# Reordering the first token chunk of a fused attention and MLP kernel: a later load of the last w_out quarter, output tiles kept open, AV items in score banks

## Chip, cores, metric

One core of one Trainium2 chip. The metric is device time of one launch, in microseconds (us). Ratios are the mean time of one kernel's fast runs over the mean of the other's fast runs of the same rounds on the same chip, so they are not quite the ratio of the medians quoted. Each has a 95% interval. One run of the kernel before (334.01 us) did not count as fast. "PE" is TensorE's matmul row of the profile, "ACT" ScalarE, "DVE" VectorE, "POOL" GpSimd, "SP" the queue that issues output stores.

## The reference, cut

```python
# q, k, v: (8 batches, 8 heads, 576, 64); s: (8, 8, 576)
scores = q @ k.T / 8 ; bias = -(cumsum(relu(s))_i - cumsum(relu(s))_j) ; causal mask
attn   = softmax(scores + bias) @ v            # per batch and head
x      = attn as (4608 tokens, 512)
h      = x @ w_in                              # 512 x 2048
g      = 0.5 * h * (1 + erf(h / sqrt(2)))
out    = g @ w_out                             # 2048 x 512
```

## The kernel before: the parts that matter

Tokens go through the MLP in nine chunks of 512. Between the output matmuls of chunk c (`l2_item`: 128 matmuls, 4 output tiles of 128 tokens, 16 steps each) the kernel runs the attention of batch c+1 (here "pair" p means heads 2p and 2p+1):

- `tr_items`: PE transposes of q and k, copied out by ScalarE and VectorE;
- `sc_item`: scores, exp on ScalarE (1.02 us each, two per pair), causal masks on VectorE;
- `av_item`: the product with v (numerator `num`) and with the decay weights (denominator `den`), then ln and exp of the denominator on ScalarE and the product into `xT` on VectorE.

The kernel shares the 8 banks of PSUM among three kinds of tile: "sc" (2 tiles of 2 banks, here called score banks), "av" (3 of one), "mlp" (1).

```python
def av_item(b, p, wide=False, rest=True):
    num, den = av_banks(wide)          # wide: both halves of one "sc" tile
    if wide:
        av_mm(b, p, num, MAIN, False)
    av_mm(b, p, den, MAIN, True)
    ln = norm_act(den, CUT, CHUNKS)    # ScalarE: ln, ln, exp
    if not wide:
        av_mm(b, p, num, MAIN, False)
    ...
    norm_dve(b, p, p + 1, num, ln, 0, CUT, CHUNKS)   # VectorE, into xT
...
def l2_item(c, sub, f0=0, f1=FT, av=False, copy=None):
    if f0 == 0:
        tag, bufs = ("av", 3) if av else ("mlp", 1)
        o_of[c, sub] = ps.tile([128, KO * 128], fp32, tag=tag, bufs=bufs, name="o_ps")
    ...                                 # the matmuls of steps f0 to f1
    if f1 < FT:
        return
    o_sb = work.tile([128, KO * 128], fp32, tag="osb", bufs=3, name="o_sb")
    (copy or nc.vector.tensor_copy)(o_sb, o_ps)
    nc.sync.dma_start(out=out[r0 : r0 + 128, :], in_=o_sb)
```

Around chunk 0, GpSimd also re-lays q and k of batch 2. These are four SBUF-to-SBUF copies, called `interleave`; they stand ahead of this stretch in program order and start when the loads are in:

```python
        if c == 0:
            load_v(2)
            interleave(2, "q")         # two GpSimd copies 128 x 1152 bf16
            interleave(2, "k")         # two more
```

Of the kernel before, what the change touches and what calls it, by code (L numbers as in the profile page):

```python
# [19 lines left out]
def kernel(  # L20
# [10 lines left out]
    nc = tc.nc  # L31
# [64 lines left out]
    def early_tile(b, n, p):  # L96
        key = "qk"[p // 2] if b < 2 else n
        if (b, key) not in early:
            early[b, key] = work.tile([128, 2, 2, G * D], bf16, tag=f"raw{key}", bufs=3, name=f"early_{key}")
        return early[b, key], (int(n == "k") if b < 2 else p // 2) * 64  # L100

    def load_early(b, n, p):
        src = q if n == "q" else k
        t, e0 = early_tile(b, n, p)
        nc.gpsimd.dma_start(
            out=t[e0 : e0 + 64].rearrange("g j e f -> g (j e) f"),
            in_=bass.AP(
                tensor=src.tensor,
                offset=src.offset + (b * H + 2 * p) * S * D,
                ap=[[G * D, 64], [S * D, 4], [1, G * D]],  # L110
            ),
        )
# [75 lines left out]
    def write_rows(b, i, eng):  # L188
        rows_of[b, i] = t = dram.tile([2, 2, S, 128], bf16, name=f"rows{b}_{i}")
        eng.dma_start(  # L190
            out=t.rearrange("j a (g r) c -> (a g) j (r c)", r=G),
            in_=qk_of.pop((b, i)).rearrange("p j r e d -> p j (r e d)"),
        )
# [283 lines left out]

    CHUNKS = [(0, 0, 256), (1, 256, CUT)]

    def av_item(b, p, wide=False, rest=True):  # L480
        num, den = av_banks(wide)
        if wide:
            av_mm(b, p, num, MAIN, False)
        av_mm(b, p, den, MAIN, True)
        ln = norm_act(den, CUT, CHUNKS)
        if not wide:
            av_mm(b, p, num, MAIN, False)
        if rest:
            av_rest(b, p)
        norm_dve(b, p, p + 1, num, ln, 0, CUT, CHUNKS)  # L490
# [44 lines left out]
    def l2_item(c, sub, f0=0, f1=FT, av=False, copy=None):  # L535

        gT = gT_of[c]
# [3 lines that stand above are left out]
        o_ps = o_of[c, sub]  # L541
        for ft in range(f0, f1):
            for e in range(2):
                t0 = sub * 128 + e * 64
                nc.tensor.matmul(  # L545
                    o_ps[e * 64 : e * 64 + 64], lhsT=gT[:, ft, t0 : t0 + 64], rhs=w_out_r[:, ft, :],
                    start=(ft == 0), stop=(ft == FT - 1), skip_group_check=True,
# [5 lines that stand above are left out]
        r0 = c * NB + sub * 128  # L553
        nc.sync.dma_start(out=out[r0 : r0 + 128, :], in_=o_sb)
# [56 lines left out]
    nc.gpsimd.tensor_copy(pace, w_in_r[:, 0, 0:1])  # L611
    for n in "qk":
        load_early(1, n, 0)
    for i in range(4):
        load_w(1, i)
    load_v(1)
    for n in "qk":
        load_early(1, n, 2)
    load_qk(2)
    avs = {p: av_banks(p < 2, p == 3) for p in (2, 0, 1, 3)}  # L620
    for p in (2, 0, 1, 3):
# [9 lines left out]
    for c in range(NCH):  # L631
        nb = c + 1
        for k0, k1 in ((0, 2), (2, 3)) if c == 0 else ((0, 3),):
            l1_item(c, 0, k0, k1)
            l1_item(c, 1, k0, k1)
        l1_item(c, 0, KO - 1)
        l1_item(c, 1, KO - 1)
        l1_item(c, 2, av=True)
        if 0 < c and nb < B:
            scale_v(nb, STS, nc.vector)  # L640
            absmax_v(nb)
        if c == 0:
            absmax_v(0)
            scale_v(0, STS[ST - 1 :], nc.vector)
        if c < B:
            for p in range(NP):
                absmax(c, p)
        if 1 < c and nb + 1 < B:
            nc.gpsimd.tensor_copy(pace, qkT[nb % 2][:, 1, NP - 1, 0:1])
            load_v(nb + 1)  # L650
            if nb + 2 < B:
                load_qk(nb + 2)
        for f2 in range(3, FT // 2):
            l1_item(c, f2)
        if c == 0:
            load_v(2)
            interleave(2, "q")
            interleave(2, "k")
            for p in range(NP):
                av_rest(0, p)  # L660
            tr_items(1, 0, (0, 1), wide=True)
            tr_items(1, 1, (0, 1), (nc.scalar.copy, nc.vector.tensor_copy), wide=True)
            exp_set()
            l2_item(c, 0, 0, 4)
            l2_item(c, 1, 0, 4, av=True)
            norm_rest(0)
            l2_item(c, 0, 4, 8)
            sc_item(1, 0)
            l2_item(c, 1, 4, 8, av=True)
            l2_item(c, 0, 8, 12)  # L670
            sc_item(1, 1)
            l2_item(c, 1, 8, 12, av=True)
            l2_item(c, 2, 0, 8, av=True)
            l2_item(c, 0, 12, copy=nc.scalar.copy)
            l2_item(c, 1, 12, av=True)
            scale_pair(1, 0)
            scale_pair(1, 1)
            l2_item(c, 2, 8, av=True, copy=nc.scalar.copy)
            av_item(1, 0, rest=False)
            l2_item(c, 3, 0, 4)  # L680
            tr_items(1, 2, (0, 1), (nc.scalar.copy, nc.vector.tensor_copy), wide=True)
            tr_items(1, 3, (0, 1), (nc.scalar.copy, nc.vector.tensor_copy), wide=True)
            scale_pair(1, 2)
            av_item(1, 1, rest=False)
            scale_pair(1, 3)
            l2_item(c, 3, 4, 8)
            sc_item(1, 2)
            l2_item(c, 3, 8, 12)
            sc_item(1, 3)
            write_rows(2, 0, nc.sync)  # L690
            av_item(1, 2, wide=True, rest=False)
            write_rows(2, 1, nc.sync)
            l2_item(c, 3, 12)
            av_item(1, 3, rest=False)
            for p in (0, 1):
                transpose_rows(2, p)
            gelu_set()
            for p in (2, 3):
                transpose_rows(2, p)
            nc.gpsimd.tensor_copy(pace, qkT[0][:, 1, 3, 0:1])  # L700
            load_qk(3)
            load_v(3)
            absmax_v(1)
        elif nb < B:
            exp_set()
            l2_item(c, 0, 0, 4)
            if c == 1:
                for p in range(NP):
                    av_rest(1, p)
            sc_item(nb, 0)  # L710
            if c == 1:
                norm_rest(1)
            l2_item(c, 0, 4)
            late = c < 3
            for p in range(1, NP):
                if nb + 1 < B and p == 1 and not late:
                    interleave(nb + 1, "q")
                    write_rows(nb + 1, 0, nc.sync)
                if nb + 1 < B and p > 1 and not late:
                    transpose_rows(nb + 1, p - 2)  # L720
                sc_item(nb, p)
                av_item(nb, p - 1)
                if nb + 1 < B and p == NP - 1 and late:
                    interleave(nb + 1, "k")
                    write_rows(nb + 1, 1, nc.sync)
                l2_item(c, p, 0, 12)
                if p == NP - 1:
                    if nb + 1 < B:
                        for pt in range(0 if late else p - 1, NP):
                            transpose_rows(nb + 1, pt)  # L730
                    if c == 1:
                        nc.gpsimd.tensor_copy(pace, qkT[(nb + 1) % 2][:, 1, p, 0:1])
                        load_qk(nb + 2)
                    av_item(nb, p)
                    norm_rest(nb)
                    gelu_set()
                l2_item(c, p, 12)
                if nb == B - 1 and p == 1:
                    cert_decay()
                if nb + 1 < B and p == 2 and late:  # L740
                    interleave(nb + 1, "q")
                    write_rows(nb + 1, 0, nc.sync)
                if nb + 1 < B and p == 1 and not late:
                    interleave(nb + 1, "k")
                    write_rows(nb + 1, 1, nc.sync)
        else:
            if c == B - 1:
                cert_1()
            for sub in range(4):
                if c == NCH - 1 and sub == 2:  # L750
                    break
                l2_item(c, sub, av=sub % 2 == 0)
                if c == B - 1 and sub < 3:
                    (cert_2, cert_3, cert_4)[sub]()
# [174 lines left out]
```

## Time and profile before

| | before |
|---|---|
| median (range), 6 runs | 327.62 us (326.76 to 334.01) |
| span of the profiled run | 324.7 us |
| PE busy | 316.0 us (97%) |
| layer 1 of chunk 0 starts at | 20.31 us |
| layer 1 of chunk 1 starts at | 57.95 us |
| layer 1 of chunk 2 starts at | 92.97 us |

All that the change touches lies between the first and the last of these three starts. I call that distance, 72.66 us here, "the stretch", and use it to compare profiles. From layer 1 of chunk 2 to the start of the last group of matmuls every profile agrees: 220.50 us before, 220.51 after, 220.50 to 220.52 in all the runs below.

### The profile page before, as it was taken

To read this page: it belongs to the slowest core of one execution; us is meant where nothing else is said; L and a number is where in the kernel's file an instruction comes from. 1 tells how busy PE (TensorE), PEld (TensorE's weight loads), DVE (VectorE), ACT (ScalarE), POOL (GpSimd) and SP (SyncE) were. 2 spreads that over 40 slices of the span, in tenths; PEclk is the share of its full clock that TensorE was granted. 3 is DMA by queue.
4 is the path that set the end of the run, shared out by engine and by line. 5 is a ranking of instruction groups with operands and counts; after the bars stand their busy time and mean duration, and the time that the engine had idled before them with its cause. 6 is when DMAs were issued, how large, how long until landed. Compare 5 with 4: busy or idle time off the path is not lost.

```text
span 324.7 us, 8755 instructions
## 1 busy us (share of the span) xinstructions
PE 316.0 (97%) x3755; PEld 183.9 (57%) x3755; DVE 191.1 (59%) x376; ACT 205.0 (63%) x292; POOL 69.8 (21%) x104
## 2 busy tenths in 40 slices
PE   8999998999999999999999999999999999999994
PEld 3666555666655556556655665556555655555554
DVE  6777547995579257936494749655883673150011
ACT  3896749758676857677667767677759676204500
POOL 8745253504300460007105300500000000000000
PEclk9999999999999999999999999999999999999999
DMA  7999999854985799968997996645500110010012
GB/s 113 219 207 209 234 191 266 266 110 51 261 256 112 108 225 253 185 109 250 222 223 145 214 239 141 166 139 177 129 15 34 63 38 2 33 66 34 1 69 71
DMA packets 53837, 47.45 MB, mean 146 GB/s; under 512 B 31328, under 2 KB 43872, under 8 KB 53792
## 3 DMA queue, kind: packets, MB, share of 16 engines
q0 software_dynamic: 15936, 23.07, 39.2%
q1 hardware_dynamic: 37856, 23.75, 27.3%
q8 instruction: 31, 0.51, 0.6%
q14 instruction: 14, 0.11, 0.1%
HBM read 36.85 MB, written 16.52 MB: 164 GB/s over the span
## 4 chain that ended last, share of the span: by engine, by line
PE 81%; DMA 11%; POOL 4%; ACT 2%; issue 1%; DVE 0%; POOLq 0%; DVEq 0%
PE h_ps L523 34%; PE o_ps L545 33%; DMA w_out_r<-in_moe_w_out_dram 5%; PE sc_ps L388 4%; PE avd L426 4%; DMA early_k<-in_k_dram 4%; PE avn L426 3%; DMA w_in_r<-in_moe_w_in_dram 3%; PE lo_ps L769 2%; PE avr L426 1%; POOL raw_v L205 1%; ACT P L404 1%; POOL early_q L117 1%; POOL early_k L117 1%; POOL w_out_r L250 0%
## 5 line engine op out<-in xcount | busy, mean ns | idle before, releaser
L523 PE MATMUL h_ps<-xT,w_in_r 128*64 128x512 bf16 x1152 | 126.2, 379 | 0.1
L545 PE MATMUL o_ps<-w_out_r,gT 128*64 128x512 bf16 x1088 | 125.9, 380 | 0.0
L523 PEld LDWEIGHTS <-w_in_r 128*64 128x64 bf16 x1152 | 68.5, 110 | 55.8 <-issue 0.7
L530 ACT ACTIVATE gT<-h_ps 128x1024 bf16<-128x1024 f32 x54 | 54.3, 1023 | 52.2 <-PE h_ps L523 52.2
L545 PEld LDWEIGHTS <-gT 128*64 128x64 bf16 x1088 | 59.2, 110 | 48.3
L404 ACT ACTIVATE P<-sc_ps 128x1024 bf16<-128x1024 f32 x64 | 62.1, 1021 | 26.2 <-PE sc_ps L388 25.0
L413 DVE TENSOR_TENSOR P<-P,tri_bf 128x512 bf16<-128x512 bf16 x58 | 24.2, 423 | 43.6 <-ACT P L404 43.2
L552 DVE COPY o_sb<-o_ps 128x512 f32<-128x512 f32 x32 | 22.0, 687 | 46.3 <-PE o_ps L545 46.3
L216 DVE TENSOR_REDUCE amx<-qkT 128x2 f32<-128x1152 bf16 x32 | 40.9, 1334 | 0.0
L205 POOL DMA_DIRECT2D raw_v<-in_v_dram x40 | 34.7, 918 | 8.5 <-DMA early_q<-in_q_dram 2.4
L462 DVE SCALAR_TENSOR_TENSOR xT<-avn,ln 128x256 bf16<-128x256 f32 (+3 forms) x66 | 22.4, 386 | 21.3 <-ACT ln L443 15.5
L233 DVE TENSOR_TENSOR vv<-raw_v,wb 128x512 bf16<-128x512 f32 (+3 forms) x44 | 25.2, 630 | 0.0
L223 DVE TENSOR_REDUCE amv<-raw_v 128x1 f32<-128x2048 f32 (+1 forms) x16 | 23.0, 1469 | 2.4 <-DMA raw_v<-in_v_dram 2.4
L443 ACT ACTIVATE ln<-ln 128x512 f32<-128x512 f32 (+1 forms) x40 | 23.5, 587 | 1.3
L533 ACT ACTIVATE gT<-h_ps 128x512 bf16<-128x512 f32 x36 | 19.6, 602 | 6.3 <-PE h_ps L523 6.3
L442 ACT ACTIVATE ln<-avd 128x256 f32<-128x256 f32 x58 | 19.2, 391 | 6.3 <-PE avd L426 6.3
L388 PE MATMUL sc_ps<-qkT 64*128 64x256 bf16 (+2 forms) x320 | 21.1, 250 | 0.7 <-ACT P L404 0.7
L388 PEld LDWEIGHTS <-qkT 64*128 64x128 bf16 x320 | 13.1, 94 | 15.1 <-issue 13.1
L426 PEld LDWEIGHTS <-wb 128*64 128x64 bf16 x384 | 17.1, 110 | 3.9 <-issue 0.3
L426 PEld LDWEIGHTS <-vv 128*64 128x64 bf16 x384 | 17.7, 110 | 1.8 <-issue 1.0
L426 PE MATMUL avd<-P,wb 128*64 128x256 bf16 x232 | 16.5, 263 | 0.0
L426 PE MATMUL avn<-P,vv 128*64 128x256 bf16 x232 | 16.0, 260 | 0.0
(101 smaller groups left out, 164.8 us busy)
## 6 DMA issues: line engine op xcount, KB each, us to landing
out_dram<-o_sb SPq DMA_DIRECT2D x34, 256.0 KB, 3.3
raw_v<-in_v_dram POOLq DMA_DIRECT2D x32, 256.0 KB, 8.6
rows<-qk_bf SPq DMA_DIRECT2D x12, 576.0 KB, 5.9
early_q<-in_q_dram POOLq DMA_DIRECT2D x13, 288.0 KB, 10.3
early_k<-in_k_dram POOLq DMA_DIRECT2D x13, 288.0 KB, 11.7
w_in_r<-in_moe_w_in_dram POOLq DMA_DIRECT2D x4, 512.0 KB, 11.4
w_out_r<-in_moe_w_out_dram POOLq DMA_DIRECT2D x4, 512.0 KB, 15.0
raw_v<-in_v_dram POOLq DMA_DIRECT2D x8, 128.0 KB, 10.2
```

The costliest lines, as they stand in the source:

```text
L205: nc.gpsimd.dma_start(out=t[:n_st, st, :, :], in_=bass.AP(tensor=v.tensor, offset=v.offset + b * H * S * D + st * 128 * D, ap=[[D, n_st], ...
L216: nc.vector.tensor_reduce(amx[:, b * NP + p], qkT[b % 2][:, :, p, :S], axis=AX, op=ALU.max, apply_absolute_value=True)
L223: nc.vector.tensor_reduce(amv[:n_st, b, j : j + 1], t[:n_st, st0:st1].rearrange("p s h d -> p (s h d)"), axis=AX, op=ALU.max, apply_absolu ...
L233: eng.tensor_tensor(vb[:n_st, st0:st1, h0:h1, :], t[:n_st, st0:st1, h0:h1, :], wb[:n_st, st0:st1, b * H + h0 : b * H + h1] .unsqueeze(3).t ...
L388: nc.tensor.matmul(s_ps[:, e, off : off + n], lhsT=qkT[b % 2][e * 64 : e * 64 + 64, 1, p, jt * 128 : jt * 128 + 128], rhs=qkT[b % 2][e * 6 ...
L404: nc.scalar.activation(P[:, :, UO[u] : UO[u] + UW[u]], s_ps[:, :, : UW[u]], func=AF.Exp, scale=scale)
L413: eng.tensor_tensor(d, d, tri_bf.unsqueeze(1).unsqueeze(1).to_broadcast([128, 2, 2, 128]), op=MULT)
L426: nc.tensor.matmul(out[e * 64 : e * 64 + 64, lo : lo + n], lhsT=(wb[:, jt, b * H + h : b * H + h + 1].to_broadcast([128, 64]) if den else ...
L443: nc.scalar.activation(ln[:, :w], ln[:, :w], func=AF.Exp, scale=-1.0)
L523: nc.tensor.matmul(h_of[c, f2][i][e * 64 : e * 64 + 64], lhsT=w_in_r[:, ko, ft * 128 + e * 64 : ft * 128 + e * 64 + 64], rhs=xT[:, ko, c * ...
L530: nc.scalar.activation(gT_of[c][:, f2 * 2 : f2 * 2 + 2, :], hh_of[c, f2], func=AF.Gelu)
L545: nc.tensor.matmul(o_ps[e * 64 : e * 64 + 64], lhsT=gT[:, ft, t0 : t0 + 64], rhs=w_out_r[:, ft, :], start=(ft == 0), stop=(ft == FT - 1), ...
```

## The change

Intent: have v and the last q and k of batch 1 earlier by loading w_out's last quarter behind them. Then use that: run AV of pairs 0 and 1 sooner in score banks, keep all four output tiles of chunk 0 open, and spend their last steps as filler where TensorE waited for ScalarE.

```diff
-    def av_item(b, p, wide=False, rest=True):
+    def av_item(b, p, wide=False, rest=True, den_first=None):
         num, den = av_banks(wide)
-        if wide:
+        den_first = not wide if den_first is None else den_first
+        if not den_first:
             av_mm(b, p, num, MAIN, False)
         av_mm(b, p, den, MAIN, True)
         ln = norm_act(den, CUT, CHUNKS)
-        if not wide:
+        if den_first:
             av_mm(b, p, num, MAIN, False)
@@
-    for i in range(4):
+    for i in range(3):
         load_w(1, i)
     load_v(1)
-    for n in "qk":
-        load_early(1, n, 2)
+    for p in (2, 3):
+        for n in "qk":
+            load_pair(1, n, p)
+    load_w(1, 3)
     load_qk(2)
@@
             l2_item(c, 1, 8, 12, av=True)
-            l2_item(c, 2, 0, 8, av=True)
-            l2_item(c, 0, 12, copy=nc.scalar.copy)
-            l2_item(c, 1, 12, av=True)
+            l2_item(c, 2, 0, 12, av=True)
             scale_pair(1, 0)
             scale_pair(1, 1)
-            l2_item(c, 2, 8, av=True, copy=nc.scalar.copy)
-            av_item(1, 0, rest=False)
-            l2_item(c, 3, 0, 4)
+            av_item(1, 0, wide=True, rest=False, den_first=True)
+            l2_item(c, 3, 0, 4, av=True)
+            av_item(1, 1, wide=True, rest=False, den_first=True)
+            l2_item(c, 3, 4, 8, av=True)
             tr_items(1, 2, ...)              # cut: arguments unchanged
             tr_items(1, 3, ...)
             scale_pair(1, 2)
-            av_item(1, 1, rest=False)
+            l2_item(c, 3, 8, 12, av=True)
+            sc_item(1, 2)
             scale_pair(1, 3)
-            l2_item(c, 3, 4, 8)
-            sc_item(1, 2)
-            l2_item(c, 3, 8, 12)
+            l2_item(c, 0, 12)
+            l2_item(c, 1, 12, av=True)
             sc_item(1, 3)
+            l2_item(c, 2, 12, av=True)
             write_rows(2, 0, nc.sync)
             av_item(1, 2, wide=True, rest=False)
+            l2_item(c, 3, 12, av=True)
             write_rows(2, 1, nc.sync)
-            l2_item(c, 3, 12)
             av_item(1, 3, rest=False)
```

## The prediction

> **What bounds the kernel now.** I read the summary page, then a table of engine busy time by stretch, then the chain of waits, then TensorE's, VectorE's and GpSimd's timelines between 34 and 62 us, then the DMA view in short stretches.
>
> The page and the table by stretch (columns: stretch, its length, then busy us of PE, PEld, DVE, ACT, POOL, granted clock, DMA share, GB/s):
>
> ```profile
> PE 316.0 (97%) x3755; PEld 183.9 (57%) x3755; DVE 191.1 (59%) x376; ACT 205.0 (63%) x292; POOL 69.8 (21%) x104
> ...
> 30.00:40.00 10.00, 9.74 (x188) 6.16 (x186) 6.49 (x8) 7.01 (x10) 3.45 (x5) 1.00 1.23 226
> 40.00:50.00 10.00, 9.94 (x136) 5.49 (x135) 4.59 (x12) 5.41 (x9) 5.14 (x8) 1.00 1.15 200
> 50.00:60.00 10.00, 8.84 (x170) 6.05 (x160) 9.01 (x22) 9.49 (x16) 4.91 (x6) 1.00 0.98 240
> 80.00:90.00 10.00, 10.00 (x134) 6.27 (x132) 5.64 (x16) 6.04 (x10) 4.40 (x6) 1.00 1.10 241
> ```
>
> TensorE is the bound: 8.7 us of the 324.7 us span lack a matmul, and most of these lie before the first matmul (1.2) and after the last (about 4). What the change can reach is the stretch from 34.9 to 58.7 us: the output matmuls of token chunk 0, with batch 1's transposes, scores and AV products between them. Only there is PE short of full; from 60 us it runs at 10.00 of 10. VectorE (9.01) and ScalarE (9.49) are nearly full in 50 to 60 us, too.
>
> The chain of waits through that stretch (start, length, what):
>
> ```profile
> 21.89 15.86 DMA w_out_r<-in_moe_w_out_dram
> 37.76 0.28 issue
> 38.04 11.66 DMA early_k<-in_k_dram
> ...
> 52.68 2.83 ACT P L404 x3
> 55.51 0.04 issue
> 55.55 0.96 PE avw L426 x16
> ...
> 58.24 0.43 DVE xT L462
> 58.67 0.04 issue
> 58.71 13.57 PE h_ps L523 x124
> ```
>
> The third w_out quarter lands at 37.75; its arrival lets GpSimd issue the last k load, which lands at 49.70. The transposes (at 49.75) then wait for it, but PE reached them at 49.47, so that wait is only 0.2 us deep. Behind it ScalarE is the link, to 55.5. TensorE's timeline shows the gaps:
>
> ```profile
> 53.74 0.39 PE L388 MATMUL sc_ps<-qkT 64*128 64x256 bf16 x4
> 54.64 0.40 PE L388 MATMUL sc_ps<-qkT 64*128 64x256 bf16 x6 [0.50 <-ACT P L404]
> 55.55 0.57 PE L426 MATMUL avw<-P,vv 128*64 128x256 bf16 x8 [0.52 <-ACT P L404]
> ```
>
> The prize: from 34.88 to 57.95 is 23.1 us. Its work: 128 output matmuls at 0.108 us in a row (56 take 6.06) is 13.8; four score items at 0.55 is 2.2; four AV items at 0.77 is 3.1; four transposes at about 0.5 is 2.0. Sum 21.1, so 2.0 us of slack, plus some 0.3 us that the next first-layer matmuls lose before 58.71 for pair 2's xT. At most 2.3 us of 327, 0.7%, can be won.
>
> **What the Trainium skill says.** "Perfetto Trace Analysis", section "Identifying the Most-Contended Engine": matmul busy is no measure of distance to roofline. Agreed here (PEld 57%); I use only the gaps. "SBUF — State Buffer", section "Who interferes with whom": a VectorE instruction with two SBUF inputs contends with a GpSimd instruction that reads SBUF, and the later one blocks until the other ends. The trace agrees: the 128x128 mask takes 218 ns at the median of 29, but 1168 ns once, beside a GpSimd copy:
>
> ```profile
> 56.79 1.17 DVE L418 TENSOR_TENSOR P<-P,tri_bf 128x128 bf16<-128x128 bf16 x1
> 56.65 2.31 POOL L181 COPY qk_bf<-early_q 128x1152 bf16<-128x1152 bf16 x2 [3.47 <-DMA early_q<-in_q_dram]
> ```
>
> "DMA: Bandwidth & Descriptors", section "Queues, rings and completion order": each DMA engine takes turns between queues that have work. It agrees: with output stores in flight (first two lines, 50 to 53 us) the input queue gets 62% of the engines; without them (last two, 55 to 57 us) 109%.
>
> ```profile
> q0 software_dynamic: 286, 0.37, 62.3%
> q1 hardware_dynamic: 280, 0.51, 50.2%
> q0 software_dynamic: 210, 0.41, 109.2%
> q1 hardware_dynamic: 3, 0.00, 1.0%
> ```
>
> **The change part by part.** No matmul, exp or byte is added; work is reordered. Two more DMA issues (0.66 us each on GpSimd) and two o_sb copies that go from ScalarE (0.59 each) to VectorE (0.69).
>
> (1) Loads. In before, quarters of w_out land at intervals of 2.5 to 2.8 us (GpSimd's waits end at 32.99, 35.52, 38.04, 40.85). With the last one moved behind v and k, v of batch 1 comes about 2.7 us sooner (last piece about 45 rather than 47.5) and the last k about 47 rather than 49.7. The fourth quarter takes over k's place, 49.5 to 50, since the bytes ahead of it are the same. Gone: the 0.2 us at the transposes.
>
> (2) Order on TensorE, worked from 41.68 (end of scores 1,1; same in both) with the durations above. Output 1 and 2: 32 matmuls, 3.46, to 45.14. AV(1,0) to 45.9; 8 outputs to 46.8; AV(1,1) to 47.55; 8 outputs to 48.4; transposes pair 2 to 49.0. Pair 3's need the score bank that AV(1,1) now occupies, free after its ln and exp (1.3) and two VectorE products (0.76): 47.35 + 1.35 + 0.8 = 49.5, so about 0.5 us of new wait; done 50.05. Eight outputs to 50.9; scores(1,2) to 51.45. Now w_out's last quarter is needed, 1.5 us after it lands. 16 outputs to 53.2 (ScalarE's two exps of 1.02 finish then, so nearly no wait); scores(1,3) to 53.8; 8 outputs to 54.6; AV(1,2) to 55.5; 8 outputs to 56.3. The 0.50 and 0.52 us waits of before are thus filled. If AV(1,3) could run at once, layer 1 would start at 57.1 and the gain be about 1 us.
>
> (3) VectorE, which now gets the evacuations late and in one heap. Its order after the pair 3 transposes (built program): scale(1,2) to 51.8; masks(1,2), held by the exps, to 53.85; scale(1,3) 0.87 to 54.7; o_sb 0 and 1 to 55.95; masks(1,3) 0.85 to 56.8; o_sb 2 to 57.45; xT(1,2) 0.75 to 58.2; o_sb 3; xT(1,3). AV(1,3) needs its masks, and its numerator needs the bank of output 2: 57.5 to 57.9. Layer 1 starts at 57.9 and gets pair 2's xT at 58.25, against 57.95 and 58.71. That is 0.4 us gained without any collision.
>
> (4) Collision with GpSimd. The output stores no longer run at 46 to 54, so the input queue regains what they took: (1.1 - 0.62) x 3 + (1.1 - 0.78) x 2 + about 0.3, over 1.1, or 2 us (0.78 is its share from 53 to 55 us). GpSimd's four copies (4.6 us in all), which began at 56.65 when q of batch 2 was in, begin at about 54.6. Masks(1,3), at 56, are then wholly beside them, and each of three can wait out a copy of 1.14 us; before, one did (0.95 lost). Estimate: 0.5 to 3 us lost, 1.5 in the middle.
>
> (5) Store of output 0. The o_sb pool has three buffers, so copy 3 waits for store 0. Store 0 now leaves at 55.4, not 46:
>
> ```profile
> out_dram<-o_sb SPq DMA_DIRECT2D x3, 256.0 KB, 6.3
> ```
>
> Those were the stores at 45 to 50 us, beside full input traffic. At 5 to 6 us store 0 lands about 61; copy 3 and xT(1,3) end at 62.4. Layer 1 wants pair 3's xT after 24 matmuls, 57.9 + 2.6 = 60.5. Up to 1.9 us of stall; it lies beside the loss of (4), not on top of it.
>
> Sum: -0.4 from the order, plus the larger of (4) and (5), some 1.5: about +1 us. The two undisturbed runs of before are 326.98 and 327.7, mean 327.3. I say 328.1: a little under 328.3, because the two collisions depend on half a microsecond each.
>
> **The rivals.** First, the intended gain: VectorE keeps up, GpSimd's copies come later than the masks, and the stretch loses 1 to 1.5 us: 326.0. For it: PE's waits on ScalarE are real, and (2) fills them. Against: VectorE's heap. Second, the last w_out quarter comes late: a quarter took 12.3 to 16.2 us from issue to landing; issued at about 41 it could land at 57, and output 0 would wait up to 5 us: 332. Against: that latency is queueing behind loads which are the same bytes. Third, nothing: only what ScalarE delays changes place, 327.3.
>
> **Range and chances.** 326.2 to 330.0 holds rival one, rival three and most of (4) and (5). A gain of 2% (6.5 us) is beyond the 2.3 us of slack: 0.01. A loss of 2% needs w_out over 6 us late, or a median made of slow runs like the 334.01: 0.02.
>
> **What would show it.** Right: no wait at the k transposes; about 0.5 us before pair 3's; copies o_sb in a heap at 54 to 58; masks(1,3) of over 1 us beside GpSimd copies; copy 3 waiting on a store; layer 1 of chunk 1 starting at 58 to 60, or stalling after its 24th matmul. Wrong: PE waiting at output 0 for w_out; masks of 0.2 to 0.4 us, and layer 1 starting before 57.5, which is rival one.

## The result

| | before | after |
|---|---|---|
| median, 6 runs each | 327.62 us | 331.18 us (329.61 to 332.39) |
| ratio of fast runs | 1 | 1.0112 (1.0072 to 1.0151) |
| span of the profiled run | 324.7 us | 330.5 us |
| the stretch in it | 72.66 us | 77.83 us |

The kernel became 1.1% slower: 3.6 us where I had said under 1, and outside my range. The profiled run of after is the slowest of its six, so its 5.2 us of extra stretch is the upper end of what the runs show.

First the page's first line and the table by stretch of after (columns as in the prediction: stretch, length, busy us of PE, PEld, DVE, ACT, POOL, then granted clock, DMA share, GB/s):

```profile
PE 317.3 (96%) x3755; PEld 184.6 (56%) x3755; DVE 194.6 (59%) x378; ACT 204.1 (62%) x290; POOL 71.3 (22%) x106
...
40.00:50.00 10.00, 8.50 (x98) 5.09 (x94) 5.03 (x14) 5.24 (x9) 6.04 (x9) 1.00 1.20 192
50.00:60.00 10.00, 7.72 (x150) 4.51 (x149) 8.28 (x12) 6.34 (x9) 6.70 (x6) 1.00 0.88 178
60.00:64.00 4.00, 3.29 (x26) 2.42 (x27) 3.93 (x11) 2.36 (x4) 0.00 (x0) 0.57 0.74 276
```

Three things to see. TensorE has gaps in 40 to 50 us (8.50, before 9.94), where no loss was foreseen. It has more gaps in 50 to 60 (7.72, before 8.84). And behind these the granted clock is 0.57, where before it was 1.00 in every window listed. TensorE's own timeline names the waits:

```profile
46.07 0.57 PE L426 MATMUL avw<-P,vv 128*64 128x256 bf16 x8 [0.75 <-ACT ln L442]
48.64 0.57 PE L426 MATMUL avw<-P,vv 128*64 128x256 bf16 x8 [0.75 <-ACT ln L442]
...
60.60 0.96 PE L426 MATMUL avd<-P,wb 128*64 128x256 bf16 x8 [2.40 <-DVE P L413]
61.67 0.96 PE L426 MATMUL avn<-P,vv 128*64 128x256 bf16 x8
62.37 14.71 PE L524 MATMUL h_ps<-xT,w_in_r 128*64 128x512 bf16 x128
```

The first two are the numerators of pairs 0 and 1, each held until ScalarE has read the denominator. The third is AV of pair 3, 2.40 us late because of its masks. The profile of before already has a wait of the first kind, in batch 0, where two AV items use score tiles with the denominator first:

```profile
19.17 0.57 PE L426 MATMUL avw<-P,vv 128*64 128x256 bf16 x8 [0.42 <-ACT ln L442]
```

In after, the chain of waits shows what made the masks late (start, length, what):

```profile
54.44 0.79 DVE P L413
55.23 1.08 DVE P L418
56.32 1.08 DVE vv L233
57.40 0.39 issue
57.79 1.22 DVE vv L233
59.01 1.20 DVE o_sb L553 x2
60.21 0.67 DVE P L413 x2
```

VectorE's row has two instructions of 1.16 and 2.77 us (the last of the two masks of pair 2, and the two v scalings of pair 3), and GpSimd's row has the copies beside them:

```profile
55.16 1.16 DVE L418 TENSOR_TENSOR P<-P,tri_bf 128x128 bf16<-128x128 bf16 x1
56.24 2.77 DVE L233 TENSOR_TENSOR vv<-raw_v,wb 128x512 bf16<-128x512 f32 x2
53.75 2.49 POOL L181 COPY qk_bf<-early_q 128x1152 bf16<-128x1152 bf16 x2 [1.94 <-DMA early_q<-in_q_dram]
56.18 2.69 POOL L181 COPY qk_bf<-early_k 128x1152 bf16<-128x1152 bf16 x2
```

Undisturbed, the 512-wide mask takes 0.43 us, the 128-wide one 0.22 and the two scalings 0.88 together. So VectorE lost 0.36 + 0.94 + 1.89 = 3.2 us beside the copies, all in one row; the masks of pair 3 behind it came 3.2 us later than in run 1 below, where the copies are held.

**Theories.** A: GpSimd's copies hold up VectorE's two-input operations, and this is the larger part. B: the denominator-first order in a shared score tile is the loss. C: the heap of output copies on VectorE (1.27 us ahead of pair 3's masks). D: the load order.

### The profile page after: what moved, and what is told of

Read it like the earlier page. It is cut to its first block, busy times and chain, and to the rows that moved or that the text cites. A ratio compares the mean times of both kernels' runs of the same rounds, so it can differ in the third digit from the quotient of the medians.

```text
span 330.5 us, 8753 instructions
## 1 busy us (share of the span) xinstructions
PE 317.3 (96%) x3755; PEld 184.6 (56%) x3755; DVE 194.6 (59%) x378; ACT 204.1 (62%) x290; POOL 71.3 (22%) x106
## 4 chain that ended last, share of the span: by engine, by line
PE 91%; DVE 3%; ACT 3%; DMA 1%; issue 0%
PE h_ps L524 38%; PE o_ps L546 35%; PE sc_ps L388 5%; PE avd L426 3%; PE avn L426 3%; PE lo_ps L772 2%; ACT P L404 1%; DMA s_sw<-in_s_dram 1%; PE avr L426 1%; PE tr_ps L367 1%; PE avw L426 1%; DVE o_sb L553 1%; ACT ln L442 1%; DVE vv L233 1%; DVE P L413 0%; DVE qkT L373 0%
## 5 line engine op out<-in xcount | busy, mean ns | idle before, releaser
L553 DVE COPY o_sb<-o_ps 128x512 f32<-128x512 f32 x34 | 23.2, 685 | 44.2 <-PE o_ps L546 44.2
L462 DVE SCALAR_TENSOR_TENSOR xT<-avn,ln 128x256 bf16<-128x256 f32 (+3 forms) x62 | 20.9, 384 | 20.0 <-ACT ln L443 14.2
L233 DVE TENSOR_TENSOR vv<-raw_v,wb 128x512 bf16<-128x512 f32 (+3 forms) x44 | 27.2, 675 | 0.3
L442 ACT ACTIVATE ln<-avd 128x256 f32<-128x256 f32 x54 | 17.9, 392 | 9.2 <-PE avd L426 9.2
L426 PE MATMUL avd<-P,wb 128*64 128x256 bf16 x216 | 15.7, 268 | 2.4 <-DVE P L413 2.4
L652 POOL CAST pace<-qkT 128x1 f32<-128x1 bf16 x4 | 0.8, 198 | 69.8 <-DMA qkT<-rows 69.8
```

The costliest lines, as they stand in the source:

```text
L233: eng.tensor_tensor(vb[:n_st, st0:st1, h0:h1, :], t[:n_st, st0:st1, h0:h1, :], wb[:n_st, st0:st1, b * H + h0 : b * H + h1] .unsqueeze(3).t ...
L426: nc.tensor.matmul(out[e * 64 : e * 64 + 64, lo : lo + n], lhsT=(wb[:, jt, b * H + h : b * H + h + 1].to_broadcast([128, 64]) if den else ...
```

## Experiments

All give correct results. Each was timed in five rounds against the kernel before on its own chip. Runs 1 to 4 shared one chip; 5 to 8, 9 to 11 and 12 to 14 each another. "Stretch" is from each one's profile, which is a single run of the six: in after and in runs 2 and 14 it is the slowest or second slowest, so small differences of it say little.

| run | on top of | ratio to before (95%) | stretch, us | named PE wait before AV of pair 3 |
|---|---|---|---|---|
| before | | 1 | 72.66 | none |
| after | before | 1.0112 (1.0072 to 1.0151) | 77.83 | 2.40 |
| 1 hold copies | after | 1.0068 (1.0037 to 1.0100) | 74.90 | none |
| 2 numerator first | after | 1.0085 (1.0044 to 1.0126) | 77.41 | 2.82 |
| 3 both | after | 1.0035 (1.0006 to 1.0065) | 74.07 | none |
| 4 old loads | after | 1.0168 (1.0126 to 1.0209) | 77.32 | 0.83 |
| 5 both, 4 buffers | after | 0.9985 (0.9966 to 1.0005) | 72.88 | none |
| 6 reordered | run 5 | 0.9981 (0.9962 to 1.0000) | 72.89 | none |
| 7 hold copies | before | 0.9991 (0.9965 to 1.0016) | 73.43 | none |
| 8 ScalarE copies | after | 1.0077 (1.0055 to 1.0099) | 75.44 | 0.86 |
| 9 reordered again | run 6 | 0.9947 (0.9903 to 0.9992) | 72.19 | none |
| 10 4 buffers | after | 1.0082 (1.0034 to 1.0130) | 75.70 | 0.33 |
| 11 loads only | before | 1.0202 (1.0154 to 1.0251) | 78.43 | none |
| 12 hold, 4 buffers | after | 1.0025 (1.0002 to 1.0048) | 73.92 | none |
| 13 numerator first, 4 buffers | after | 1.0127 (1.0094 to 1.0160) | 77.11 | 2.06 |
| 14 after again | after | 1.0141 (1.0112 to 1.0171) | 78.54 | 2.68 |

**Run 1, hold the copies** (theory A).

```diff
-            interleave(2, "q")                  # ahead of the stretch
-            interleave(2, "k")
 ...
             sc_item(1, 3)
+            nc.gpsimd.tensor_copy(pace, P_of[1, 3][:, 1, PW - 1 : PW])  # last masked column
+            interleave(2, "q")
+            interleave(2, "k")
```

> The changed kernel with GpSimd's four copies for batch 2 held back until the masks of pair 3 of batch 1 are done (one tiny GpSimd copy reads the last masked column first); nothing else moves. Theory A (the copies hold up VectorE's two-input operations, and that is the larger part of the loss): the masks of pair 2 and 3 and the v scalings between 53 and 61 us go back to about 0.43, 0.22 and 0.9 us for two, TensorE's 2.4 us wait before AV of pair 3 falls below 0.5, the granted clock stays at 1.00, and the time falls by 3 to 4.5 us, to about 327.5. Rival B (the denominator-first order in a score bank is the loss): the two waits of 0.75 us stay, and the time falls by under 1 us. Rival C (VectorE's heap of output copies): the wait stays above 1.2 us.

Measured: 329.32 us median, 1.0068. VectorE's long instructions are gone, and so is the wait before AV of pair 3; layer 1 of chunk 1 starts at 58.80 us, not 62.37, and the clock is 1.00 from 60 us on. But the gain is smaller than A said: 1.9 us by the medians, 0.44% (1.4 us) by the ratios, where 3 to 4.5 were expected; and the intervals of the two ratios overlap. VectorE's and TensorE's timelines show why:

```profile
54.85 0.88 DVE L233 TENSOR_TENSOR vv<-raw_v,wb 128x512 bf16<-128x512 f32 x2
...
61.19 0.69 DVE L553 COPY o_sb<-o_ps 128x512 f32<-128x512 f32 x1 [1.77 <-DMA out_dram<-o_sb]
62.60 3.64 PE L524 MATMUL h_ps<-xT,w_in_r 128*64 128x512 bf16 x32 [0.78 <-DVE xT L462]
```

With VectorE on time, output copy 3 comes before store 0 has left its buffer (stores land after 2.4 to 4.7 us here), waits 1.77 us, and holds xT of pair 3 behind it: a new wait in place of the old one. That is step (5) of my prediction, which in after itself was hidden.

**Run 2, numerator first** (theory B): `den_first=True` dropped in both places.

> The changed kernel with the numerator ahead of the denominator in the AV items of pairs 0 and 1 of batch 1, as the other items in score banks have it. Rival B: both waits of 0.75 us on ScalarE's ln go, everything behind comes 1.5 us sooner and the time falls by 1.5 us or a little more. Theory A: the GpSimd copies keep their place in time (they start when q of batch 2 lands, about 53.8 us), so masks and scalings get ahead of part of them; the wait before AV of pair 3 falls to between 0.5 and 2 us, and the time by 1.5 to 3 us. If the time falls by under 0.7 us, the two waits were hidden behind VectorE.

Measured: 329.66 us, 1.0085; the profile's stretch fell by only 0.4. Both waits of 0.75 us are gone, yet pair 3's transposes now wait for the score bank, and the rest is eaten by the copies, which keep their place in time:

```profile
49.68 0.48 PE L367 MATMUL tr_ps<-ident_bf,early_k 64*64 64x64 bf16 x36 [1.03 <-DVE xT L462]
60.02 0.87 PE L426 MATMUL avd<-P,wb 128*64 128x256 bf16 x8 [2.82 <-DVE P L413]
```

By the ratios 0.9 us was gained, by the medians (two chips) 1.5, where both theories expected 1.5 us or more, and the wait before AV of pair 3 grew to 2.82 us, where theory A had 0.5 to 2. Work that is done sooner ran into the same obstacle.

**Run 3, both edits.**

> Both edits together. Theory A with B as a second, separate part: neither the 0.75 us waits nor the long masks are left, layer 1 of chunk 1 starts about 23 us after the end of layer 1 of chunk 0 (before: 23.1), and the time is that of the kernel before or up to 1 us less: 326.5 to 327.6. If the time stays above 328.5, a third cost (the heap of output copies) is there.

Measured: 328.13 us, 1.0035 (1.0006 to 1.0065): 0.5 us above the times expected, and 1.2 us above before on its chip, where 0 to 1 us under it was expected. On the same chip as run 1 the denominator order is now worth 0.33%, or 1.1 us. What remains above before is in the trace: 1.03 us for the score bank, and 1.67 us of VectorE waiting for store 0 (0.68 named on TensorE).

**Run 4, old load order in the changed kernel** (theory D).

> The changed kernel with the loads in the old order (last w_out quarter ahead of v, k and q of batch 1 in two loads); the order of work stays. If the load order costs or gains: over 1 us either way. Theory A and B: the k transposes come at about 50 us in this order anyway, when the old loads have just landed (49.7), and the GpSimd copies start within 0.5 us of 53.8, so the time is that of the changed kernel within 0.7 us.

Measured: 331.84 us, 1.0168. By the medians that is 0.7 us above after, by the ratios 1.8; of the four runs on its chip this is the slowest, but its interval overlaps with both timings of after (1.0112, and 1.0141 in run 14). Whether the old loads cost anything on top is therefore not shown. The trace shows other waits than I expected: I had looked at k alone; it is v that comes too late for AV of pair 0:

```profile
46.97 1.69 DVE L233 TENSOR_TENSOR vv<-raw_v,wb 128x512 bf16<-128x512 f32 x4 [3.67 <-DMA raw_v<-in_v_dram]
47.72 0.57 PE L426 MATMUL avw<-P,vv 128*64 128x256 bf16 x8 [2.81 <-DVE vv L233]
```

In after the scalings of pairs 0 and 1 started at 43.86 us without a wait. On the other side, the wait before AV of pair 3 is 0.83 us for 2.40 here. Putting the old loads back returned nothing, so the new loads are not the cause of the loss. GpSimd's copies began at 53.70 with the old loads too: their early start does not come from the new load order. (The granted clock stayed at 1.00 behind the 2.81 us wait; more on that below.)

**Run 8, output copies 0 and 1 on ScalarE** (theory C).

```diff
-            l2_item(c, 0, 12)
-            l2_item(c, 1, 12, av=True)
+            l2_item(c, 0, 12, copy=nc.scalar.copy)
+            l2_item(c, 1, 12, av=True, copy=nc.scalar.copy)
```

> The changed kernel with output copies 0 and 1 on ScalarE, as the kernel before had its copies of outputs 0 and 2; GpSimd's copies are not touched. Rival C (the heap of output copies on VectorE): VectorE loses 1.27 us ahead of pair 3's masks, the wait before AV of pair 3 falls from 2.4 to about 1.2 us, and the time by 1 to 2 us (the clock drop may go with it). Theory A: the masks and scalings stay long (over 0.75, 1.1 and 2 us) since GpSimd is still beside them, and the kernel stays at least 1.5 us slower than before.

Measured: 329.11 us, 1.0077 (1.0055 to 1.0099). As both theories had it: the wait before AV of pair 3 fell to 0.86 us and the clock held, but the masks beside the copies stayed long (the two 512-wide ones 2.48 us for 0.85):

```profile
53.37 2.48 DVE L413 TENSOR_TENSOR P<-P,tri_bf 128x512 bf16<-128x512 bf16 x2
59.06 0.69 PE L426 MATMUL avd<-P,wb 128*64 128x256 bf16 x8 [0.86 <-DVE P L413]
```

The gain against after (0.35%) is within the noise of the two ratios. The heap makes the row that the copies lengthen longer; without the collision (runs 5 and 12) the heap stays and costs no named wait of AV of pair 3.

**Run 5, both edits and four output buffers** (`tag="osb", bufs=3` to `bufs=4` on top of run 3).

> Both edits of the run before, and a fourth buffer for the output copies, so that copy 3 need not wait for store 0. In the run with both edits VectorE waited 1.67 us on the store ahead of copy 3, and layer 1 of chunk 1 stopped after its 24th matmul (0.68 us named). If that wait is real cost: it goes, the stretch between the starts of layer 1 of chunk 0 and of chunk 2 falls from 74.1 us to about 73.2 (before: 72.7), and the time to 0.1 to 0.2 % above before. Rival: another release (pair 3's ln on ScalarE) sets the same moment, and the stretch falls by under 0.3 us.

Measured: 326.35 us, 0.9985 (0.9966 to 1.0005), stretch 72.88. The store wait was real: 1.2 us of stretch against run 3. With these three edits the whole loss is gone, a little more than was expected.

**Run 7, the kernel before with the copies held.**

> The kernel before, with GpSimd's four copies held back until pair 3's masks are done. The one mask of 1168 ns returns to about 220 ns. Theory A says that it lies on the chain to layer 1 of chunk 1 by at most the 0.3 us that layer 1 loses there: the time falls by 0 to 0.4 us. If it falls by 0.9 us or more, the mask was wholly on the path. If it rises by over 0.5 us, holding the copies has a cost of its own (the q and k rows of batch 2 come later).

Measured: 326.31 us, 0.9991 (0.9965 to 1.0016): no difference clear of noise. Its long mask returned to 0.22 us, and pair 2's product still waited for ScalarE's ln at 58.30. In before one copy collides where there is slack; the same mechanism costs nothing there. (Its profiled stretch is 0.77 us longer; 0.61 of this is a wait for k that before did not have.)

**Run 11, the load order alone in the kernel before.**

> The kernel before with the new load order alone. Its output 0 wants w_out's last quarter at about 44.3 us, which now lands at about 49.5 to 50: TensorE waits 5 to 5.7 us by name, some of which the later waits of before (0.2 + 0.5 + 0.5 us) give back; the clock may drop behind a wait this long. Time 4 to 6 us above before. If it is under 2 us above, the quarter lands much sooner than taken.

Measured: 333.81 us, 1.0202, 6.8 us over before's median on its chip, more than expected. TensorE waits for the last quarter by name, and the clock falls behind it (0.91 and 0.92 in 40 to 50 and 50 to 60 us):

```profile
48.94 4.91 PE L545 MATMUL o_ps<-w_out_r,gT 128*64 128x512 bf16 x32 [4.57 <-DMA w_out_r<-in_moe_w_out_dram]
```

So the new loads can't stand alone: under the old work they cost 2.0%. Old loads under the new work (run 4) cost 1.7%, which the noise doesn't part from the cost of both together (1.1 and 1.4%).

**Run 10, four buffers alone.**

> The changed kernel with the fourth buffer for output copies alone. In its trace copy 3 did not wait for store 0 (the stores landed within 2.1 us at the median, and copy 3 was late for other reasons), so the theory says no change: within 0.3 % of the changed kernel's 1.1 % over before. If the time falls by over 1 us, the store wait of the prediction was at work in the changed kernel too.

Measured: 329.66 us, 1.0082 (1.0034 to 1.0130). No store wait in it, as in after, and the interval overlaps with that of after. In its profile the copies happened to hit other instructions (both pairs of scalings 1.83 us, one mask 1.15), and the wait was 0.33 us on the masks and 1.33 on an output copy.

**Runs 12, 13 and 14, on one chip**, to see how the loss splits between the copies and the denominator order.

> The changed kernel with the copies held and the fourth buffer; the denominator stays first. With the runs before it makes a clean two-by-two: collision present or not, denominator first or not, the store wait out of the way in all. If the two 0.75 us waits are real cost once nothing behind them hides them: 0.6 to 1.2 us above the run with both edits and four buffers, so 1.001 to 1.002 of before. If they are hidden by the score bank wait that replaces them there: within 0.3 us of it.

> The changed kernel with the numerator first and the fourth buffer; the copies are free to collide. If the collision is the larger cost: 1.006 to 1.008 of before, hardly under the changed kernel, since work that comes sooner still runs into the copies, which keep their place in time at about 53.5 us. If the denominator-first order were the larger cost: under 1.003.

> The changed kernel itself again, on the chip of the other two, as the fourth corner: 1.008 to 1.012 of before. Its profile shows whether the granted clock falls in the layer 1 of chunk 1 in every execution or only where the wait before AV of pair 3 is long.

Measured: 1.0025, 1.0127 and 1.0141. With runs 10 and 5 (each on another chip, so only the ratios compare) they make a two-by-two:

| four buffers | copies collide | copies held |
|---|---|---|
| denominator first | 1.0082 (run 10) | 1.0025 (run 12) |
| numerator first | 1.0127 (run 13) | 0.9985 (run 5) |

Holding the copies is worth 0.6% in the upper row and 1.4% in the lower; in the upper row 1.2% if run 14 (same chip, three buffers) stands in for run 10. The numerator order is worth 0.4% where the copies are held, and nothing that shows where they collide. Run 13 missed its expectation (1.006 to 1.008): with the work earlier, the collision again fell on the last mask and both scalings, and the clock fell too:

```profile
58.78 0.69 PE L426 MATMUL avd<-P,wb 128*64 128x256 bf16 x8 [2.06 <-DVE P L413]
60.48 15.44 PE L524 MATMUL h_ps<-xT,w_in_r 128*64 128x512 bf16 x128
```

Run 14 is above its expected range (1.008 to 1.012) at 1.0141, but its interval overlaps with that of the first timing. Its six spans go from 327.9 to 331.8 us, at clocks of 0.994 to 1.000.

**Runs 6 and 9, a better order.** Run 6 put pair 3's transposes behind the next eight output matmuls, output 0 ahead of scores of pair 2, output 2 ahead of scores of pair 3, and both scalings together, on top of run 5; run 9 put output 2 back behind scores of pair 3:

```diff
             tr_items(1, 2, ...)
+            l2_item(c, 3, 8, 12, av=True)
             tr_items(1, 3, ...)
             scale_pair(1, 2)
-            l2_item(c, 3, 8, 12, av=True)
-            sc_item(1, 2)
             scale_pair(1, 3)
             l2_item(c, 0, 12)
+            sc_item(1, 2)
             l2_item(c, 1, 12, av=True)
             sc_item(1, 3)          # run 6: l2_item(c, 2, 12) ahead of this line
             ...                    # the held copies of run 1
             l2_item(c, 2, 12, av=True)
```

> The run before, with pair 3's transposes put behind the next 8 output matmuls, so that their score bank is free when TensorE comes to them, output 0 ended ahead of scores of pair 2, output 2 ahead of scores of pair 3, and both v scalings together. Theory: the 1.03 us wait for the bank goes to 0.1 to 0.4; if w_out's last quarter lands by 50 us, no wait for it; the stretch between the starts of layer 1 of chunk 0 and chunk 2 is 72.0 to 72.7 us, and the time equal to before or up to 0.7 us less. If w_out's last quarter is late, TensorE waits at output 0 for it by name.

Measured for run 6: 326.16 us, 0.9981 (0.9962 to 1.0000). The score bank wait is gone, but the stretch is 72.89 us where 72.0 to 72.7 was expected, since a new wait, 0.90 us, is there at AV of pair 2:

```profile
56.83 0.57 PE L426 MATMUL avw<-P,vv 128*64 128x256 bf16 x8 [0.90 <-ACT P L404]
```

> The reordered run with output 2 behind scores of pair 3 again, where it can fill TensorE's wait for the score bank. In the reordered run scores of pair 3 came at 55.3 us, two exps behind them held the bank, and AV of pair 2 waited 0.90 us. Theory: scores of pair 3 come 0.9 us sooner, the 8 output matmuls of output 2 cover the exp, the wait falls below 0.2 us, the stretch between the starts of layer 1 of chunk 0 and 2 falls from 72.9 to about 72.2 us (before 72.7), and the time to 0.2 to 0.4 % under before. Rival: the masks of pair 3 then set the start of AV of pair 3, and the stretch stays above 72.7.

Measured for run 9: 325.60 us against 326.99 of before on its chip, 0.9947 (0.9903 to 0.9992), stretch 72.19. That AV item now starts behind eight matmuls with no wait named:

```profile
54.41 0.55 PE L426 MATMUL avw<-P,vv 128*64 128x256 bf16 x8
```

This version beats the changed kernel clearly, and the kernel before by little: one of before's eleven runs on that chip is 331.16, and without it the ratio would be 0.996; in the profiles the stretch is 0.47 us shorter. So the intent of the change was sound, for 0.1 to 0.5%, within the 0.7% that the slack allowed.

## Why the prediction was wrong

- **The bound, the slack and the class.** Right. TensorE stayed the bound, and the difference is within 2%, but the measured 331.18 us is above my 330.0. One reading was loose: TensorE is short of full in other places too (31.64 of the first 34 us are busy, and a wait of 0.79 stands before the last group of matmuls); the change doesn't reach them.
- **Step (1), loads.** Right. v of batch 1 was there when pair 0 wanted it at 43.86; w_out's last quarter landed at about 50.0 (GpSimd's next issue waited for it until 50.07), where 49.5 to 50 was said. TensorE never waited for it. Rival two is out.
- **Step (2), order on TensorE: this step failed by an omission.** I took AV of pairs 0 and 1 at 0.77 us each. With the denominator first in one tile, the numerator waits until ScalarE has read the other half: 0.75 us named, twice, and the items took 1.68 and 1.71 us. Scores of pair 3 came at 54.87, which is 55.25 counted from the same start of layer 1, against 53.2 predicted: 2.05 us late. About half of this is the denominator order: in run 5, with the numerator first, the same scores come 1.05 us sooner. The rest stays there, most of it named: the wait for pair 3's bank was 1.02 us where I had 0.5 (in after the denominator waits cover it), and VectorE's copies of the transposes hold the scores of pair 2 for 0.23 (0.49 in after), which I didn't have. The built program held the denominator wait (the first numerator matmul of both items waits on ScalarE), and before's profile had one like it (0.42 us at 19.17), so it could have been read.
- **Step (3), VectorE's row.** The order was right; the durations held in the runs with held copies. The 0.4 us that the new order was to gain without a collision is not there: in run 5, with collision, denominator wait and store wait all gone, the stretch is 0.2 us longer than before's. It took another order (run 9) to gain 0.5.
- **Step (4), the collision: right mechanism, mis-sized.** I gave 0.5 to 3 us, 1.5 in the middle, on the masks of pair 3. It measured 3.2 us, on the masks of pair 2 and the scalings of pair 3. The copies began at 53.75 (54.13 counted from the same start) rather than 54.6; the input queue had 120% of the engines from 50 to 53 us (62% before, and 110% in my estimate). VectorE's work came 2 us later than step (2) said, so more of it lay beside them. I also left out the scalings, which have two SBUF inputs like the masks. The masks of pair 3, which I had named, stayed short (0.74 us for two, and 0.21). The held copies show this as the larger part: 1.2% (run 12 against run 14) and 1.4% (run 5 against run 13), against 0.3 to 0.4% for the denominator order.
- **Step (5), the store.** It did not happen in after: copy 0 ran at 58.94, when the input queue was down to 32% of the engines (57 to 60 us), and stores landed in 2.1 us at the median. It came as soon as the collision was removed (run 1: 1.77 us), and the fourth buffer took it away. "Beside (4), not on top" was right.
- **Not foreseen: the clock.** After the 2.40 us wait the granted clock was 0.57 over 60 to 64 us (0.50 from 61 to 63), and layer 1 of chunk 1 took 14.71 us where it takes 14.01 undisturbed (runs 8 and 10). The Trainium skill, "TensorE: Matmul & The Clock Gate", section "What's actually happening", says that an idle window throttles the array to half its clock; I didn't carry it into the sum. In four profiles (after, runs 2, 13, 14), with named waits of 2.06 to 2.82 us, layer 1 of chunk 1 took 14.71 to 15.44; in runs 4, 8 and 10, with 0.33 to 0.86, it took 14.01. The length of the wait alone doesn't settle it: run 4's wait of 2.81 us before AV of pair 0, at 45 to 48 us, left the clock at 1.00.

The sum, from the profile of after, counted from the start of layer 1 of chunk 0: layer 1 of chunk 1 came 4.85 us later than step (3) had it. Of these 2.05 are from step (2). From the start of scores of pair 3 to layer 1, step (3) had 4.7 us (53.2 to 57.9), with some waiting in it; run 12, where the copies are held, took 4.00 (54.96 to 58.96), and after 7.50 (54.87 to 62.37). So the other 2.8 us, or 3.5 against run 12, are the collision: 2.6 us in which TensorE stood still before AV of pair 3 (2.40 named), and 0.9 in that item itself, 1.77 us for 0.87, at a granted clock of 0.69 and then 0.50. Layer 1 then lost another 0.7. Of the theories, A holds as the larger part; B is a true cost (0.3 to 0.4%) that the collision covers; C only lengthens the row that A delays; D falls. Single edits gave back less than their shares, as the traces have it, because each wait hid the next: denominator wait, collision, store wait. What stays open is how much of the run-to-run spread of after (329.61 to 332.39) is the clock and how much is where the copies fall among VectorE's instructions. The clock of the six runs, 0.994 to 1.000, does not order their times fully, and runs 10 and 14 differ by more than their traces explain.

## What to carry to other kernels

When work is moved on the bounding engine, list for every other engine what now runs beside what. Here nothing was added, but GpSimd copies that cost nothing clear of noise in one order cost VectorE 3.2 us in another, since they came when their load landed and not when VectorE had time. If one wait is removed and the gain doesn't come, read which wait took its place before giving up the edit: here three edits that gave 0.3 to 0.4% each when tried alone, none of it clear of the noise, took away the whole 1.1% together. And before putting two accumulations in one tile, ask which engine reads the first while the second is written.

## What the Trainium skill lacked or had wrong

- "SBUF — State Buffer", section "Who interferes with whom": right here as far as it goes. It speaks of pairs of instructions; the runs show that in a row each VectorE instruction with two SBUF inputs can wait for a copy anew (0.79 for 0.43, 1.16 for 0.22, and 2.77 for 0.88 us behind one another), while output copies from PSUM kept their 1.27 us for two beside a copy (run 10) as without one (run 12). In run 10 it also went the other way: two masks in the middle of GpSimd's second pair of copies kept their 0.74 us, and that pair took 3.07 us for its 2.23.
- "TensorE: Matmul & The Clock Gate", section "What's actually happening": it gives an idle window of about 3.4 us before the clock falls. Here the clock was 0.57 to 0.71 over 60 to 64 us behind named waits of 2.06 to 2.82 us (after, runs 2, 13 and 14), and 1.00 behind waits of 0.33 and 1.33 us (run 10), but also behind one of 2.81 us (run 4). So it fell behind waits shorter than that window, though not behind each; what parts the cases is not shown.
- No page has the cost of sharing one tile between two accumulations when another engine reads the first: here a named wait of 0.75 us in each item, which lengthens the item by 0.91 us (1.68 in run 12 for 0.77 in run 5), by the program's own wait on ScalarE, though the halves are separate banks.
- "DMA: Bandwidth & Descriptors", section "Queues, rings and completion order": turns between queues agree, and the runs add what taking stores away does: the input queue's share rose from 62% to 120% over 50 to 53 us, and GpSimd's copies of q of batch 2 began 2.9 us sooner (53.75 for 56.65), which put them beside the masks of pair 2. Run 4, with the old loads and the late stores, shows the same (118%, 53.70).
